# A fused attention and MoE kernel: maxima as bias in the head, another load order, and every third weight pair converted twice

## The chip, the cores and the metric

The kernel runs on one core of a Trainium2 chip. The metric is device time in microseconds. Before the change it is 929.2 us, the median of three runs (927.67 to 930.06).

## The reference, cut to what matters

```python
def _attn_ref(q_l, k_l, v_l, q_g, k_g, v_g):      # B 4, H 8, Sl 512, Sg 32, D 64
    s_g = scale * q_g @ k_all.T                   # 32 global queries see all 544 keys
    out_g = sm(s_g) @ v_all
    s_ll = where(|i - j| <= 32, scale * q_l @ k_l.T, -1e9)
    s_l = concat([scale * q_l @ k_g.T, s_ll])     # local queries: 32 global keys and a band
    out_l = sm(s_l) @ v_all                       # sm subtracts the row's maximum
    return concat([out_g, out_l])

def reference(...):
    x = attention, reshaped to (2176, 512)
    xn = x / sqrt(mean(x * x) + 1e-6) * rms_g
    y = (silu(xn @ w_gate) * (xn @ w_val)) @ w_out       # d_ff 1536
    h = relu(y @ w_in)
    return (s * h * h + b) @ moe2_w_out                  # d_ff 2048
```

## The kernel before, in words

The 2176 tokens are cut into five groups (GROUPS: three of 512 tokens, two of 320). A group goes through two phases. Phase 1 has 12 blocks f, each with a gate block `g`, a value block `v` and an output block `o`; phase 2 has 16 blocks, each with an input block `i` and an output block `p`. A block of weights is 128x512 and costs 12 matmuls of 512 columns (`mm3`, L705 to L708: a product is formed of three, high times high, high times low, low times high part). The blocks lie in 34 pairs (PAIRS) in the order of BLOCKS: pair 0 holds g0 and v0, pair 1 g1 and v1, pair 2 o0 and g2, pair 3 v2 and o1, and so on.

Weights come as raw 8-byte numbers, 1 MB a pair (`load_raw`, L166). In the first group each pair is converted: `conv_begin` (L184) makes the scaled high word on ScalarE (L192) and, on ScalarE and VectorE (L202, L203) or on VectorE alone (`halves`, L197 and L199), the low bits, clamps (L205) and merges them (L206); `conv_end` (L210) makes the high part on ScalarE (L213) and the low part on VectorE (L214), starts the next raw load and stores the finished pair of 1 MB to memory (L217). The later groups load the finished pairs (L242). `used` (L232) is called when a block has been used up; at the end of a pair it converts the pair four further on (C_LEAD) or loads the one five further on (W_LEAD). There are seven buffers for finished pairs and four for raw ones.

The attention of the first batch, four units (a unit is two heads), is done in the head by `start` (L572), the others between the weight matmuls in steps that a planner emits (`sched`, `tick`, `emit_step`; a step has a due time in TensorE's time). In `start`, `S_(u)` computes scores, masks the band's ends (L313), takes the maximum (L314), subtracts it (L315) and takes the exponential (L320); `T_(u)` transposes and copies; `V_(u)` multiplies with the values, forms the shares (`shares`, L333: L336 to L338), squares and sums them (L649, L652, L653). `fill` (L614) issues matmuls of ones whose result nobody reads. `first_norm` (L540) computes the norm, scales (L553, L555), transposes (L562) and writes x in two parts (L567, L568). Then the main stream of weight matmuls starts (L706).

The order on an engine in the head is set by hand with `in_line` (L173), which makes each instruction of a list follow the one before it on its engine; elsewhere in the first group a scheduler sets it from priorities (`hp`) and dependences. From the second group on, TensorE, ScalarE and VectorE keep the program's order (L766). SP issues all transfers, in the order of its queue:

```python
        ld_qk(0)
        nc.sync.dma_start(out=ct, in_=cst)
        ld_qk(1)
        ld_qk(2)
        ld_v(0)
```

Unit steps behind the head are in `pair_steps` (L345): `st_s` scores, `st_e` exponentials, `st_t` transposes, `st_v` values and shares. In phase 2 a block's result goes through relu (L812), `t` (L813), the high part of h (L815) and its remainder (L816), into one of two buffers; two PSUM banks ("m") take turns for the blocks `g`, `v` and `i`.

Of the kernel before, what the change touches and what calls it, by code (L numbers as in the profile page):

```python
# [70 lines left out]
C_LEAD = 4  # L71


@with_exitstack
def attn_moe_kernel(ctx: ExitStack, tc: tile.TileContext, q, k, v, w, cst, out):
# [39 lines left out]

    behind = mybir.DependencyInfo(mybir.DependencyClass.NoSync, mybir.DependencyReason.DATA)
# [25 lines left out]
    raws = {}  # L142
# [41 lines left out]
    def conv_begin(n, halves=False):  # L184
# [6 lines left out]
        with hp(20):  # L191
# [9 lines left out]
            else:  # L201
# [4 lines left out]
            d.append(V.scalar_tensor_tensor(out=t, in0=t, scalar=3, in1=e, op0=ALU.logical_shift_left,  # L206
                                            op1=ALU.bitwise_or))
        return g, a, d

    def conv_end(n, g):  # L210
        wn = w_tile(n)
        with hp(40):
            a = A.copy(out=wn[:, :, 0], in_=g)  # L213
            d = V.tensor_tensor(out=wn[:, :, 1], in0=g, in1=wn[:, :, 0].bitcast(F32), op=ALU.subtract)  # L214
        load_raw()
        wsc[n] = dr_p.tile([128, 2, 2, 512], F32, name=f"wsc{n}")
        nc.sync.dma_start(out=wsc[n], in_=wn.bitcast(F32))  # L217
        return a, d

    def conv(n):  # L220
# [5 lines left out]
        conv_end(n, g)  # L226

# [4 lines left out]
    def used(n):  # L232
        left[n] -= 1
        if left[n]:
            return
        del wt[n], left[n]
        if n + C_LEAD < PAIRS:
            conv(n + C_LEAD)
        while PAIRS <= nload[0] <= n + W_LEAD and nload[0] < PAIRS * len(GROUPS):
            m = nload[0]  # L240
            nload[0] += 1
            nc.sync.dma_start(out=w_tile(m).bitcast(F32), in_=wsc[m % PAIRS])  # L242
# [13 lines left out]
    def load_qk(i):  # L256
# [51 lines left out]

    def less_max(bk, pp):
        sv = bk.rearrange("p h (c n) -> p (h c) n", n=128)  # L310
        ends = sv.rearrange("p a (b n) -> p a b n", n=64)[:, :, :, 0:32]
        mx = sm_p.tile([128, 8], F32, tag="mx", name="mx")
        r = [V.tensor_tensor(out=ends, in0=ends, in1=mask, op=ALU.add)]  # L313
# [31 lines left out]
    def pair_steps(i, now):  # L345
# [78 lines left out]
        def st_v(e):  # L424
# [5 lines left out]
            if loc:  # L430
                shares(bk, u_tile(b)[:, :, 128 * (p + e):128 * (p + e) + 128])
# [108 lines left out]
    def first_norm(ss, fill):  # L540
# [9 lines left out]
        for c in range(4):  # L550
            o = ut[0][:, c]
            if c == 3:
                scaled.append(A.mul(out=o, in_=o, mul=r[:, c:c + 1]))  # L553
            else:
                scaled.append(V.tensor_scalar(out=o, in0=o, scalar1=r[:, c:c + 1], scalar2=None, op0=ALU.mult))  # L555
# [16 lines left out]
    def start():  # L572
# [50 lines left out]
        cp, ex, sq, ev, rd, am = {}, {}, {}, {}, {}, {}  # L623

        def S_(u, n=0):
# [16 lines left out]
        def V_(u):  # L642
            bk = banks(("at", "acc1", "acc0", "at")[u])
            in_turn(values(bk, window(u), lambda a, g: pts[u][:, a, 32 * g:32 * g + 32]), True)
            ev[u] = shares(bk, u0[:, :, 128 * u:128 * u + 128])
            j = tmp_p.tile([128, 4, 128], F32, tag="ta", name="s_j")
            uu = u0[:, :, 128 * u:128 * u + 128]
            if u < 2:
                sq[u] = [A.activation(out=j[:, c], in_=uu[:, c], func=AF.Square, accum_out=ss[:, c, u:u + 1])  # L649
                         for c in range(4)]  # L650
            else:
                sq[u] = A.activation(out=j, in_=uu, func=AF.Square)  # L652
                rd[u] = V.tensor_reduce(out=ss[:, :, u], in_=j, axis=mybir.AxisListType.X, op=ALU.add)  # L653
# [22 lines left out]
        g1, a1, d1 = conv_begin(1, True)  # L676
        a1e, d1e = conv_end(1, g1)
        g2, a2, d2 = conv_begin(2)
# [225 lines left out]
```

## Time and profile before

| | |
|---|---|
| median of three runs | 929.2 us |
| the profiled execution | 930.39 us |
| its span, first to last instruction | 928.6 us |
| mean granted TensorE clock | 0.989 |
| matmuls, weight loads | 6946, 6946 |
| VectorE, ScalarE busy | 434.8 us, 387.2 us |
| read from memory, written | 214.60 MB, 40.11 MB |

The profile is of one execution; 1.8 us of its time lie outside the span. Times in the views are microseconds from the span's start. A busy matmul in the rows overlaps the next, so the distance of starts, not the duration, gives the pace. "idle before" names what ended the idle time ahead of an instruction, as the trace's semaphores tell it; "issue" is a wait for nothing that the profile shows.

### The profile page before, as it was taken

How to read it: one execution, taken by the hardware profiler on the slowest of the kernel's cores; microseconds unless marked ns; L12 is line 12 of the kernel's file. 1: busy time of each engine (PE TensorE's matmuls, PEld its weight loads, DVE VectorE, ACT ScalarE, POOL GpSimd, SP SyncE). 2: the span in 40 equal slices, each digit the busy share in tenths (PEclk: the TensorE clock that was granted, in tenths of full speed). 3: DMA queues.
4: the chain of work that ended last, by engine and by line, in shares of the span. 5: the costliest groups of instructions: out<-in, count | busy, mean ns of one | idle time of the engine just before them, and what ended most of it. 6: DMA issues, size and time to landing. Idle time of an engine off the chain costs nothing.

```text
span 928.6 us, 16334 instructions
## 1 busy us (share of the span) xinstructions
PE 910.9 (98%) x6946; PEld 777.3 (84%) x6946; DVE 434.8 (47%) x754; ACT 387.2 (42%) x558; POOL 0.6 (0%) x7
## 2 busy tenths in 40 slices
PE   9799999999999999999999999999999999999998
PEld 6577887878878878888878878887899999999998
DVE  5898889979642242334251332344222235311333
ACT  2797997979424115233214115231232233211322
POOL 0000000000000000000000000000000000000000
PEclk7999999999999999999999999999999999999999
DMA  9999999986976675564585655554588787798880
GB/s 359 404 404 424 365 426 422 395 341 277 393 266 220 257 252 181 211 238 179 181 297 205 235 209 182 179 193 151 194 323 305 277 291 272 248 338 303 289 300 29
DMA packets 43960, 255.77 MB, mean 275 GB/s; under 512 B 5104, under 2 KB 9456, under 8 KB 15984
## 3 DMA queue, kind: packets, MB, share of 16 engines
q1 hardware_dynamic: 43888, 254.73, 73.5%
q8 instruction: 55, 0.90, 0.4%
q14 instruction: 17, 0.14, 0.0%
HBM read 214.60 MB, written 40.11 MB: 274 GB/s over the span
## 4 chain that ended last, share of the span: by engine, by line
PE 92%; ACT 3%; DVE 3%; DMA 1%; issue 1%; SPq 0%; ACTq 0%; DVEq 0%
PE m L706 16%; PE m L707 16%; PE m L708 16%; PE acc L706 12%; PE acc L707 12%; PE acc L708 12%; PE at L289 1%; PE at L329 1%; PE at L324 1%; PE at L374 1%; PE at L408 1%; ACT cv L192 1%; PE at L494 1%; DMA wr<-in_w_dram 1%; DMA s_k<-in_k_dram 1%
## 5 line engine op out<-in xcount | busy, mean ns | idle before, releaser
L707 PE MATMUL acc<-h,wt 128*128 128x512 f32 (+1 forms) x536 | 193.6, 361 | 0.8 <-DVE h L816 0.8
L708 PE MATMUL acc<-h,wt 128*128 128x512 f32 (+1 forms) x536 | 192.4, 359 | 0.0
L706 PE MATMUL acc<-h,wt 128*128 128x512 f32 (+1 forms) x536 | 187.0, 364 | 3.2 <-ACT h L815 2.8
L706 PE MATMUL m<-x,wt 128*128 128x512 f32 (+1 forms) x480 | 174.1, 363 | 0.2 <-ACT sg L783 0.2
L708 PE MATMUL m<-x,wt 128*128 128x512 f32 (+1 forms) x480 | 171.6, 358 | 0.0
L707 PE MATMUL m<-x,wt 128*128 128x512 f32 (+1 forms) x480 | 171.6, 357 | 0.0
L706 PE MATMUL m<-y,wt 128*128 128x512 f32 (+1 forms) x320 | 115.7, 362 | 2.7 <-DVE t L813 2.7
L706 PEld LDWEIGHTS acc<-h,wt 128*128 128x128 f32 x536 | 100.9, 189 | 17.8 <-ACT h L815 4.1
L707 PE MATMUL m<-y,wt 128*128 128x512 f32 (+1 forms) x320 | 115.3, 360 | 0.3 <-DVE y L743 0.3
L708 PE MATMUL m<-y,wt 128*128 128x512 f32 (+1 forms) x320 | 114.9, 359 | 0.0
L707 PEld LDWEIGHTS acc<-h,wt 128*128 128x128 f32 x536 | 101.0, 189 | 14.4 <-DVE h L816 2.1
L708 PEld LDWEIGHTS acc<-h,wt 128*128 128x128 f32 x536 | 101.1, 189 | 12.8
L795 DVE TENSOR_TENSOR a<-sg,m 128x512 f32<-128x512 f32 (+1 forms) x60 | 36.4, 606 | 158.8 <-PE m L708 147.3
L813 DVE SCALAR_TENSOR_TENSOR t<-m,ct,r 128x512 f32<-128x512 f32 (+1 forms) x80 | 53.6, 670 | 119.3 <-ACT r L812 118.9
L706 PEld LDWEIGHTS m<-x,wt 128*128 128x128 f32 x480 | 90.0, 188 | 13.5 <-issue 1.6
L812 ACT ACTIVATE r<-m 128x512 f32<-128x512 f32 (+1 forms) x80 | 42.4, 533 | 140.1 <-PE m L708 139.7
L708 PEld LDWEIGHTS m<-x,wt 128*128 128x128 f32 x480 | 90.1, 188 | 11.6
L707 PEld LDWEIGHTS m<-x,wt 128*128 128x128 f32 x480 | 90.2, 188 | 11.0 <-DVE x L568 0.2
L783 ACT ACTIVATE sg<-m 128x512 f32<-128x512 f32 (+1 forms) x60 | 32.0, 534 | 138.5 <-PE m L708 138.4
L815 ACT ACTIVATE h<-t,ct 128x512 fp32r<-128x512 f32 (+1 forms) x79 | 52.3, 662 | 54.6 <-DVE t L813 49.8
L816 DVE SCALAR_TENSOR_TENSOR h<-t,ct,h 128x512 fp32r<-128x512 f32 (+1 forms) x79 | 53.1, 673 | 46.2 <-ACT h L815 46.2
L153 ACT CAST h<-a 128x512 fp32r<-128x512 f32 (+1 forms) x55 | 30.6, 556 | 94.6 <-DVE a L795 94.6
(159 smaller groups left out, 980.2 us busy)
## 6 DMA issues: line engine op xcount, KB each, us to landing
wt<-wsc SPq DMA_DIRECT2D x136, 1024.0 KB, 4.9
wr<-in_w_dram SPq DMA_DIRECT2D x34, 1024.0 KB, 9.2
wsc<-wt SPq DMA_DIRECT2D x34, 1024.0 KB, 8.8
vr<-in_v_dram SPq DMA_DIRECT2D x12, 1105.0 KB, 8.0
fk<-in_k_dram SPq DMA_DIRECT2D x12, 784.0 KB, 6.3
fq<-in_q_dram SPq DMA_DIRECT2D x12, 272.0 KB, 6.8
out_dram<-z SPq DMA_DIRECT2D x12, 256.0 KB, 5.8
s_v<-in_v_dram SPq DMA_DIRECT2D x2, 1040.0 KB, 8.9
```

The source lines that it names most:

```text
L153: A.copy(out=out_, in_=in_)
L192: mul = lambda: A.mul(out=g, in_=hi.bitcast(F32), mul=W_SC)
L289: mms.append(PE.matmul(bk[32 * g:32 * g + 32, h, 128 * c:128 * c + 128].rearrange("p (a n) -> p a n", a=2), lhsT=qr[x, SG + 32 * i:SG + 32 ...
L706: mms = [PE.matmul(out_, lhsT=wh, rhs=xh, start=first, stop=False), PE.matmul(out_, lhsT=wh, rhs=xl, start=False, stop=False), PE.matmul(o ...
L707: PE.matmul(out_, lhsT=wh, rhs=xl, start=False, stop=False),
L708: PE.matmul(out_, lhsT=wl, rhs=xh, start=False, stop=last)]
L783: recent["A"] = A.activation(out=sg[:, :N], in_=gb[:, :N], func=AF.Silu)
L795: V.tensor_tensor(out=a[:, :N], in0=sg[:, :N], in1=vb[:, :N], op=ALU.mult)
L812: A.activation(out=r[:, :N], in_=hb[:, :N], func=AF.Relu)
L813: V.scalar_tensor_tensor(out=t[:, :N], in0=hb[:, :N], scalar=ct[:, C_S:C_S + 1], in1=r[:, :N], op0=ALU.mult, op1=ALU.mult)
L815: recent["A"] = A.activation(out=h[:, 0, :N], in_=t[:, :N], func=AF.Identity, bias=ct[:, C_B:C_B + 1])
L816: recent["V"] = V.scalar_tensor_tensor(out=h[:, 1, :N], in0=t[:, :N], scalar=ct[:, C_B:C_B + 1], in1=h[:, 0, :N].bitcast(F32), op0=ALU.add ...
```

## The change

- `S_` for units 0, 1 and 2: the subtraction goes; the maximum times -0.125 is the bias of eight exponentials of 128 columns each, which read the scores' bank. No filling stands ahead of unit 2's scores.
- Loads: raw pair 0 is issued behind q and k of unit 1, v of all four units behind q and k of unit 3. Raw pair 2 waits for the 21st value matmul of unit 3 (`vm[3][20]`); raw pair 3 and pair 0's store follow it on SP's queue, and q and k of the next batch follow raw pair 4.
- `V_`: units 0 to 2 are squared whole on ScalarE and summed on VectorE, unit 3 half on each. All four scalings are VectorE's, and the filling ahead of the first transposes is four instead of six.
- The third pair is converted as a whole behind the first silu. The orders of ScalarE and VectorE in the head are written anew.
- Pairs 4, 7, ..., 31 (AGAIN) are not stored in the first group. In the second they are loaded raw again, converted in seven steps that `tick` emits between the others (`conv_steps`), and stored then for the last three groups.
- `st_v`: the shares follow the latest remainder (`recent["V"]`). The planner's first unit step in the first group comes 12 us after the start instead of 10.

```diff
+AGAIN = range(4, PAIRS - 2, 3)
+RAW = list(range(PAIRS)) + [PAIRS + n for n in AGAIN]
...
     def load_raw():
-        n = nraw[0]
-        if n < PAIRS:
+        if nraw[0] < len(RAW):
+            n = RAW[nraw[0]]
             nraw[0] += 1
             wraw[n] = wr_p.tile([128, 2, 512], I64, tag="wr", name="wr")
-            raws[n] = nc.sync.dma_start(out=wraw[n], in_=w[n])
+            raws[n] = nc.sync.dma_start(out=wraw[n], in_=w[n % PAIRS])
...
+    def keep(n, wn):
+        m = n % PAIRS
+        if n == m and m in AGAIN:
+            return
+        wsc[m] = dr_p.tile([128, 2, 2, 512], F32, name=f"wsc{m}")
+        stores[n] = nc.sync.dma_start(out=wsc[m], in_=wn.bitcast(F32))
...
+    def conv_steps(n):
...
+        def end():
+            V.tensor_tensor(out=wn[:, :, 1], in0=g, in1=wn[:, :, 0].bitcast(F32), op=ALU.subtract)
+            load_raw()
+            keep(n, wn)
+
+        return [(lambda: A.mul(out=g, in_=hi.bitcast(F32), mul=W_SC), 0.0),
+                (lambda: A.copy(out=e.bitcast(I16), in_=odd), 1.3),
+                (lambda: V.tensor_scalar(out=g, in0=g, scalar1=-W_HI * W_SC, scalar2=W_HI * W_SC, op0=ALU.max,
+                                         op1=ALU.min), 0.6),
+                (lambda: V.tensor_scalar(out=e, in0=e, scalar1=13, scalar2=-0x7FFFFFF9, op0=ALU.arith_shift_right,
+                                         op1=ALU.bitwise_and), 1.3),
+                (lambda: V.scalar_tensor_tensor(out=t, in0=t, scalar=3, in1=e, op0=ALU.logical_shift_left,
+                                                op1=ALU.bitwise_or), 0.6),
+                (lambda: A.copy(out=wn[:, :, 0], in_=g), 1.3), (end, 1.3)]
...
         if n + C_LEAD < PAIRS:
             conv(n + C_LEAD)
+        elif n + W_LEAD in RAW[PAIRS:]:
+            sched["c"] += conv_steps(n + W_LEAD)
...
             if i < 2:
-                in_line([raws[3], d])
+                in_line([raws[4], d])
...
             if loc:
-                shares(bk, u_tile(b)[:, :, 128 * (p + e):128 * (p + e) + 128])
+                r = shares(bk, u_tile(b)[:, :, 128 * (p + e):128 * (p + e) + 128])
+                if "V" in recent:
+                    in_line([recent["V"], r])
...
         ld_qk(1)
+        load_raw()
         ld_qk(2)
-        ld_v(0)
         ld_qk(3)
-        ld_v(1)
-        ld_v(2)
-        load_raw()
-        ld_v(3)
+        for u in range(4):
+            ld_v(u)
...
+        def S_(u):
             bk = banks(("acc0", "at", "acc1", "acc0")[u])
-            if n:
-                fill(bk[:, 0], n)
             in_turn(first_scores(bk, raw[u][0], raw[u][1]), True)
-            am[u] = less_max(bk, P[u % 3])
-            ex[u] = expo(P[u % 3])
+            if u == 3:
+                am[u] = less_max(bk, P[u % 3])
+                ex[u] = [expo(P[u % 3])]
+                return
+            sv = bk.rearrange("p h (c n) -> p (h c) n", n=128)
+            mx = sm_p.tile([128, 8], F32, tag="mx", name="mx")
+            am[u] = [mask_ends(sv), V.tensor_reduce(out=mx, in_=sv, axis=mybir.AxisListType.X, op=ALU.max),
+                     V.tensor_scalar(out=mx, in0=mx, scalar1=-0.125, scalar2=None, op0=ALU.mult)]
+            ex[u] = [A.activation(out=P[u % 3][:, a], in_=sv[:, a], func=AF.Exp, scale=0.125, bias=mx[:, a:a + 1])
+                     for a in range(8)]
...
-            S_(2, 1)
+            S_(2)
...
-            roots, r, scaled, xa, xd = first_norm(sm, lambda b: fill(b, 6))
+            roots, r, scaled, xa, xd = first_norm(sm, lambda b: fill(b, 4))
...
-        g2, a2, d2 = conv_begin(2)
-        in_line([ex[0], ex[1]] + cp[0] + [ex[2]] + cp[1] + [ex[3]] + cp[2] + sq[0] + [a0[0]] + cp[3] + sq[1]
-                + [a1[0], a0e, sq[2], a2[0], sq[3], a1e] + roots + [scaled[3]] + xa + [a2[1]])
-        in_line([am[0], am[1], am[2], am[3], ev[0], d0[0], d0[1], d0[2], d0[3], ev[1], d1[0], d1[1], ev[2], d1[2], d1[3], ev[3],
-                 rd[2], rd[3], sums, r[0], r[1]] + scaled[:3] + [d0e] + xd + [d1e, d2[0], d2[1], d2[2]])
-        begun.append(d2[2])
-        ending.append(lambda: conv_end(2, g2))
+        tc.add_manual_dep(raws[2].ins, vm[3][20].ins.name, landed, reason="after")
+        in_line([raws[2], raws[3], stores[0]])
+        in_line(ex[0] + a0 + ex[1] + cp[0] + ex[2] + cp[1] + [a0e] + ex[3] + cp[2] + cp[3] + sq[0] + sq[1] + sq[2] + a1
+                + sq[3] + roots + xa + a1e)
+        in_line(am[0] + d0[:2] + am[1] + [d0[2]] + am[2] + [d0[3]] + am[3] + [d0e, ev[0], ev[1], ev[2]] + rd[0]
+                + [d1[0], ev[3]] + rd[3] + rd[1] + rd[2] + [sums, d1[1], r[0], r[1]] + scaled + [d1[2]] + xd
+                + [d1[3], d1e[0], d1[4], d1e[1]])
+        begun.append(d1e[1])
+
+        def third_pair(sg):
+            g2, a2, d2 = conv_begin(2)
+            in_line([a1e[1], sg] + a2)
+            in_line([d1e[1]] + d2)
+            conv_end(2, g2)
+
+        ending.append(third_pair)
...
         if s["q"] and s["t"] >= s["ok"] and not s["hold"] and (gap or len(s["q"][0]) < 3):
             emit_step()
+            s["cok"] = max(s["cok"], s["t"] + (3.0 if gap else 0.7))
+        elif s["c"] and s["t"] >= s["cok"]:
+            s["c"].pop(0)[0]()
+            s["cok"] = s["t"] + (s["c"][0][1] if s["c"] else 0.0)
...
-            sched["ok"] = sched["t"] + (0.0 if gi else 10.0)
+            sched["ok"] = sched["t"] + (0.0 if gi else 12.0)
...
             if ending:
-                in_line([recent["A"], ending.pop(0)()[0]])
+                ending.pop(0)(recent["A"])
                 conv(C_LEAD - 1)
```

## Rows read from the trace of the kernel before

**Rows 1.** The page, part 1: engine, busy us, share of the span, instructions.

```profile
PE 910.9 (98%) x6946; PEld 777.3 (84%) x6946; DVE 434.8 (47%) x754; ACT 387.2 (42%) x558; POOL 0.6 (0%) x7
```

**Rows 2.** Stages: busy us of PE, PEld, DVE, ACT, POOL; clock, DMA share, GB/s.

```profile
18.20:28.30 10.10, 6.98 (x230) 6.11 (x231) 7.36 (x11) 6.92 (x16) 0.00 (x0) 1.00 1.02 417
...
31.90:42.00 10.10, 8.32 (x53) 4.38 (x45) 8.86 (x21) 9.54 (x15) 0.00 (x0) 1.00 1.02 416
...
42.00:100.00 58.00, 57.42 (x375) 45.56 (x374) 51.74 (x71) 48.97 (x49) 0.00 (x0) 1.00 1.01 409
...
250.00:440.00 190.00, 190.00 (x1430) 154.73 (x1429) 67.81 (x119) 57.70 (x89) 0.00 (x0) 1.00 0.64 231
```

**Rows 3.** TensorE's waits, 42 to 245 us: total us, times, longest us.

```profile
PE m L706 <- DVE t L813: 2.7, 2, 2.1
```

**Rows 4.** Timelines of ScalarE, VectorE and TensorE around 206 us: start, duration.

```profile
198.87 0.60 ACT L812 ACTIVATE r<-m 128x512 f32<-128x512 f32 x1 [0.95 <-PE m L708]
...
205.50 0.17 DVE L336 TENSOR_SCALAR rs<-at 128x8 f32<-128x8 f32 x1 [1.52 <-PE at L408]
...
207.62 0.74 DVE L813 SCALAR_TENSOR_TENSOR t<-m,ct,r 128x512 f32<-128x512 f32 x1
...
208.41 0.50 PE L706 MATMUL m<-y,wt 128*128 128x512 f32 x1 [2.11 <-DVE t L813]
```

**Rows 5.** Chain that ended last, 196 to 214 us: start, duration, what.

```profile
209.75 0.43 PE m L707
...
213.02 0.92 PE acc L706 x4
```

**Rows 6.** Timeline of TensorE in the head and at the main stream's start.

```profile
27.40 0.30 PE L329 MATMUL acc<-s_v,ptf 128*32 128x65 f32 x3 [3.12 <-issue]
...
33.68 0.22 PE L329 MATMUL at<-s_w,ptf 128*32 128x65 f32 x1 [1.54 <-issue]
...
34.03 5.42 PE L615 MATMUL acc<-ones 128*128 128x512 f32 x12
...
41.96 0.71 PE L706 MATMUL m<-x,wt 128*128 128x512 f32 x2
```

**Rows 7.** DMA queues, 27.4 to 33.68 us: packets, MB, share of 16 engines.

```profile
q8 instruction: 1, 0.02, 1.1%
```

**Rows 8.** Timeline of VectorE and ScalarE in the head.

```profile
8.67 1.22 DVE L315 TENSOR_TENSOR pm<-acc,mx 128x1024 f32<-128x1024 f32 x1
...
9.93 1.06 ACT L320 ACTIVATE pm<-pm 128x1024 f32<-128x1024 f32 x1 [7.91 <-DVE pm L315]
...
26.00 0.30 ACT L649 ACTIVATE s_j<-u 128x128 f32<-128x128 f32 x1
...
34.95 0.16 DVE L336 TENSOR_SCALAR rs<-at 128x8 f32<-128x8 f32 x1
...
37.85 0.30 ACT L542 ACTIVATE r<-ss,epsc 128x4 f32<-128x4 f32 x1
```

**Rows 9.** Timeline behind the main stream's start: first silu, third pair's first matmuls.

```profile
47.31 0.60 ACT L783 ACTIVATE sg<-m 128x512 f32<-128x512 f32 x1 [2.93 <-PE m L708]
...
54.06 1.21 PE L706 MATMUL acc<-h,wt 128*128 128x512 f32 x4 [0.34 <-ACT h L153]
```

**Rows 10.** Groups by line, 40 to 260 us: count, busy us, mean ns, idle before.

```profile
L202 ACT COPY ce<-wr 128x2048 int16<-128x2048 int16 x31 | 58.8, 1896 | 0.0
...
L206 DVE SCALAR_TENSOR_TENSOR cv<-cv,ce 128x1024 int32<-128x1024 int32 x32 | 39.1, 1223 | 0.5
L192 ACT ACTIVATE cv<-wr 128x1024 f32<-128x1024 f32 x32 | 36.9, 1154 | 0.0
L213 ACT CAST wt<-cv 128x1024 fp32r<-128x1024 f32 x32 | 33.6, 1050 | 6.5 <-DVE cv L206 6.5
...
L205 DVE TENSOR_SCALAR cv<-cv 128x1024 f32<-128x1024 f32 x32 | 22.1, 690 | 5.7 <-ACT cv L192 5.6
```

**Rows 11.** Groups by line on ScalarE, 250 to 440 us, columns as above.

```profile
L815 ACT ACTIVATE h<-t,ct 128x512 fp32r<-128x512 f32 x13 | 9.4, 724 | 11.4 <-DVE t L813 11.4
```

More of the change, by code (lines that the diff above doesn't have):

```diff
@@ L141, in attn_moe_kernel @@
     wt, wraw, wsc, left = {}, {}, {}, {}
-    raws = {}
+    raws, stores = {}, {}
     nraw = [0]
@@ L205, in conv_begin, with conv_end @@
             d.append(V.tensor_scalar(out=g, in0=g, scalar1=-W_HI * W_SC, scalar2=W_HI * W_SC, op0=ALU.max, op1=ALU.min))
-            d.append(V.scalar_tensor_tensor(out=t, in0=t, scalar=3, in1=e, op0=ALU.logical_shift_left,
-                                            op1=ALU.bitwise_or))
+            for x in parts(split):
+                d.append(V.scalar_tensor_tensor(out=t[:, x], in0=t[:, x], scalar=3, in1=e[:, x],
+                                                op0=ALU.logical_shift_left, op1=ALU.bitwise_or))
         return g, a, d
-    def conv_end(n, g):
+    def keep(n, wn):
[4 more added lines that the diff above has]
+        stores[n] = nc.sync.dma_start(out=wsc[m], in_=wn.bitcast(F32))
+    def conv_end(n, g, split=False):
         wn = w_tile(n)
+        a, d = [], []
         with hp(40):
-            a = A.copy(out=wn[:, :, 0], in_=g)
-            d = V.tensor_tensor(out=wn[:, :, 1], in0=g, in1=wn[:, :, 0].bitcast(F32), op=ALU.subtract)
+            for x in parts(split):
+                a.append(A.copy(out=wn[:, x, 0], in_=g[:, x]))
+                d.append(V.tensor_tensor(out=wn[:, x, 1], in0=g[:, x], in1=wn[:, x, 0].bitcast(F32), op=ALU.subtract))
         load_raw()
-        wsc[n] = dr_p.tile([128, 2, 2, 512], F32, name=f"wsc{n}")
-        nc.sync.dma_start(out=wsc[n], in_=wn.bitcast(F32))
-        return a, d
+        keep(n, wn)
+        return (a, d) if split else (a[0], d[0])
     def conv(n):
@@ L241, in used @@
             nload[0] += 1
+            if m in RAW:
+                continue
             nc.sync.dma_start(out=w_tile(m).bitcast(F32), in_=wsc[m % PAIRS])
@@ L307, in first_scores, with mask_ends @@
         return mms
+    def mask_ends(sv):
+        ends = sv.rearrange("p a (b n) -> p a b n", n=64)[:, :, :, 0:32]
+        return V.tensor_tensor(out=ends, in0=ends, in1=mask, op=ALU.add)
     def less_max(bk, pp):
         sv = bk.rearrange("p h (c n) -> p (h c) n", n=128)
-        ends = sv.rearrange("p a (b n) -> p a b n", n=64)[:, :, :, 0:32]
         mx = sm_p.tile([128, 8], F32, tag="mx", name="mx")
-        r = [V.tensor_tensor(out=ends, in0=ends, in1=mask, op=ALU.add)]
+        r = [mask_ends(sv)]
         V.tensor_reduce(out=mx, in_=sv, axis=mybir.AxisListType.X, op=ALU.max)
@@ L551, in first_norm @@
             o = ut[0][:, c]
[L552 to L555, printed above, removed]
+            scaled.append(V.tensor_scalar(out=o, in0=o, scalar1=r[:, c:c + 1], scalar2=None, op0=ALU.mult))
         X[0] = xy_p.tile([128, 2, HP, NMAX], F32R, tag="x", name="x")
@@ L643, in V_ @@
             bk = banks(("at", "acc1", "acc0", "at")[u])
-            in_turn(values(bk, window(u), lambda a, g: pts[u][:, a, 32 * g:32 * g + 32]), True)
+            vm[u] = values(bk, window(u), lambda a, g: pts[u][:, a, 32 * g:32 * g + 32])
+            in_turn(vm[u], True)
             ev[u] = shares(bk, u0[:, :, 128 * u:128 * u + 128])
-            j = tmp_p.tile([128, 4, 128], F32, tag="ta", name="s_j")
+            j = pg[:, 0:512] if u == 3 else pms[1].rearrange("p a n -> p (a n)")[:, 512 * (u % 2):512 * (u % 2) + 512]
+            j = j.rearrange("p (c n) -> p c n", c=4)
             uu = u0[:, :, 128 * u:128 * u + 128]
-            if u < 2:
+            if u == 3:
                 sq[u] = [A.activation(out=j[:, c], in_=uu[:, c], func=AF.Square, accum_out=ss[:, c, u:u + 1])
[L650 to L653, printed above, removed]
+                         for c in range(2)]
+                rd[u] = [V.scalar_tensor_tensor(out=j[:, c], in0=uu[:, c], scalar=1.0, in1=uu[:, c], op0=ALU.mult,
+                                                op1=ALU.mult, accum_out=ss[:, c, u:u + 1]) for c in range(2, 4)]
+                return
+            sq[u] = [A.activation(out=j, in_=uu, func=AF.Square)]
+            rd[u] = [V.tensor_reduce(out=ss[:, :, u], in_=j, axis=mybir.AxisListType.X, op=ALU.add)]
         acc_p.append(ctx2.enter_context(tc.tile_pool(name="ph", bufs=1, space=PSUM)))
```

22 lines of the change are left out of this document (16 added, 6 removed).

## The prediction

> **What bounds the kernel now.** I read the page first: TensorE is busy for 98% of the span [rows 1]. The table by stage shows that behind the head nothing but TensorE's own work is left over: between 250 and 440 us it is busy for all 190.00 us, ScalarE and VectorE for only 57.70 and 67.81 us [rows 2]. In the first group, up to about 245 us, these two convert the weights and are nearly as full as TensorE (48.97 and 51.74 of 58 us between 42 and 100 us). So time can be won in two places alone: before the main stream of weight matmuls starts (41.96 us [rows 6]), and where TensorE stands still behind that.
>
> For the second place I read TensorE's waits from 42 to 245 us. The longest kind is 2.7 us, for VectorE's `t` on L813 [rows 3]. The timeline around the longest one shows how it comes about [rows 4]. ScalarE has finished a relu at 199.47, so its `t` could run then; but VectorE's next instructions in order are conversion steps and L336, the first step of an attention unit's shares, which waits until 205.50 for TensorE's value matmuls. `t` runs at 207.62, and TensorE, whose two banks are full, stands for 2.11 us until 208.41. Behind that, seven matmuls go at 0.43 us each, against 0.92 us for four, 0.23 each, at the usual pace [rows 5]: the half level of the clock, 1.2 GHz. That is 7 x 0.20 = 1.4 us more, so the whole event costs 3.5 us.
>
> For the first place the timeline of TensorE in the head shows two waits put down to "issue" [rows 6]: 3.12 us until 27.40 in the second unit's value matmuls, and 1.54 us until 33.68. Between the two resumptions lie 6.28 us and 3 + 8 + 64 + 53 = 128 matmuls (three of unit two, the transposes, unit three, unit four so far), and just one instruction transfer of the profile's queue 8 [rows 7]. I read this as instructions that arrive 128 matmuls at a time, no faster than once in 6.3 us while the transfer engines are full (DMA share 1.02 [rows 2]). The fourth unit's last value matmul ends at 33.95; VectorE's shares, sums and norm follow.
>
> **The change, part by part.** *Maxima as bias.* For three units VectorE loses the subtraction of 1.22 us and gains a scaling of eight numbers, 0.16 us as L336: 1.06 us less each [rows 8]. ScalarE's exponential of 1.06 us becomes eight of 128 columns. Their price lies between 1.06 us (same elements, no cost of their own) and 8 x 0.43 = 3.4 us (0.30 us for L542 with a bias from memory on 4 columns, and 0.13 us for 128 columns, an eighth of L320). I take the nearest row, a square of 128 columns, 0.30 us: 2.4 us. So a unit's chain does not get shorter (1.22 + 1.06 = 2.3 us now, 0.16 + 2.4 = 2.6 us then); 3.2 us leave VectorE and 4.0 us come to ScalarE. Both have room before 27 us, since TensorE is the one held there: 0.
>
> *Raw pair third, no filling.* A pair of 1.05 MB takes 2.5 us at 417 GB/s [rows 2], so the third unit's q and k land 2.5 us later, and a filling of about 2 us ahead of its scores goes. The two nearly cancel, and the instruction supply sets the later end, not the scores: 0.
>
> *Raw pairs 2 and 3 held until the last unit's 21st value matmul.* What is loaded ahead of them, 9 MB, takes at least 21.5 us at that rate, so the transfer engines run empty near 25 us. The first issue wait should stay, because its block is asked for while loads still run (two fill matmuls fewer move the boundary by two). The second should go, because its block comes over an empty queue. From 27.4 us on, three units' work is left: 1.3 us of transposes, 1.6 and 1.6 us of values at the half clock that follows such a wait, 0.1 us of handover. That ends near 32.0 instead of 33.95: **-2.0 us** (bounds 0, if the second wait stays, and -3.2, at the full clock). On SP's queue raw pairs 2 to 4, the first store and the next batch's q and k stand behind this hold. Pair 2 lands some 5 us after its issue near 31, and ScalarE wants it at 46; q and k are wanted only after the 12 us that the planner now keeps free.
>
> *Tail to the first matmul.* Today the shares start at 34.95 [rows 8], 1.0 us after the last value matmul, behind a conversion step; from there to the first main matmul it is 7.0 us. New: 0.2 us of handover (-0.8), two products with sums of 0.3 us more, a conversion step that sticks out by 0.2 us beside ScalarE's two small steps, and the fourth scaling on VectorE, 0.2 us: **+0.2 us**. First main matmul: 41.96 - 2.0 + 0.2 = 40.2. Filling: six of them take 5.42 us [rows 6], four 3.6 us; the transposes start some 5.6 us after the last value matmul, so TensorE idles for 2.0 us ahead of the main stream. After the wait of 1.54 us the clock stayed full (1.00 from 31.9 to 42 us [rows 2]), after that of 2.11 us it fell; between 0 and 1.4 us I take the middle: **+0.7 us**.
>
> *Third pair converted wholly behind the first silu.* Today its preparation lies in the head, and TensorE waits 0.34 us for its first use, 12.1 us after the main stream's start [rows 9]. New, from the silu's start 5.35 us after that point: 0.60 + 1.90 + 1.15 us on ScalarE, 0.69 + 1.22 us on VectorE, 1.05 us on ScalarE [rows 9, 10] make 12.0, with handovers 12.3 us. TensorE's 48 matmuls of the first two pairs are through after 48 x 0.227 = 10.9, with a bank wait of 0.4 us 11.3. It waits 1.0 us instead of 0.3: **+0.6 us** (bounds 0, if the first silu comes earlier, and +3.9, if the next pair's copy of 1.90 us goes first and the clock falls for 1.4 us).
>
> *Shares forced behind the latest remainder.* The new line in the value step puts `t` and L816 ahead of L336 on VectorE, which is the event of 3.5 us: **-3.5 us** (bounds -3.5 and 0, if the new order builds another one).
>
> *Every third pair kept raw.* Ten stores of 1 MB leave the first group, ten loads of equal size change their source. No wait of TensorE there is for a transfer: 0. The second group gets ten conversions, 10 x 4.1 us on ScalarE and 10 x 3.8 us on VectorE (two steps of 0.69 as L205, two of 1.22 as L206 [rows 10]), in a stage where both are idle for over 120 us of 190. The relu's chain (0.60, 0.74, 0.72, 0.74 us [rows 4, 11]) takes 2.8 us, and 24 matmuls, 5.4 us, pass before TensorE needs its end; one copy of 1.90 us in the way fits into the 2.6 us left: 0. Without that cover see the third rival.
>
> Sum: -2.0 + 0.2 + 0.7 + 0.6 - 3.5 = **-4.0 us**. The profiled execution lasted 930.39 us, 1.2 us over the median of 929.2; the sum on it gives 926.4, on the median **925.2 us**. Differences under 0.3%, 2.8 us, can't be told from none: faster means under 926.4, slower over 932.0.
>
> **The rivals.** (1) *The event comes back in another place.* The first group is ordered by a scheduler, and every moved instruction moves its list; with one event of 3.5 us the time is 928.7. For it: 2.7 us of waits are of this one kind, on a VectorE nearly full. Against: the forced order covers shares now as it did scores. Chance 0.24. (2) *Both issue waits go.* The fourth unit then ends near 28, 4 us sooner than in my sum: 921.2. For it: two fill matmuls fewer, and a queue that empties early. Against: the loads before 25 us are as dense as now. Chance 0.10. The Trainium skill ("Runtime: NRT & Kernel Launch", Instruction fetch mechanics) says that an engine fetches its next block while it executes the current one, and that this is mostly hidden; by it this rival would be the rule, at 921.2, and the trace's waits of 3.12 and 1.54 us speak against it. (3) *Slower: the second group's conversions get into the relu chain.* Four of the ten fall into its second half. If a copy of 1.90 us holds up the relu and a step of 1.22 us each holds up `t` and the remainder, the delay is 4.3 us against a cover of 2.6: 1.7 us, four times 6.8 us, and if the clock falls behind two of them 2.8 us more: 925.2 + 9.6 = 934.8. It decides once both engines are hit for the same block. Against it: both reach these steps early, with half their time idle. Chance 0.16.
>
> **Numbers.** Forecast 0.50, rivals 0.24, 0.10 and 0.16. The range of 920.5 to 931.5 holds the forecast with its bounds and rivals 1 and 2, and leaves out rival 3. Most of the forecast (0.45) and rival 2 are faster, the rest of it (0.05) and rival 1, less a hundredth, are the same; rival 3 and that hundredth are slower: 0.55, 0.28, 0.17. The forecast's own range is 922 to 928.
>
> **What would show it.** First main matmul near 40 us; one issue wait left in the head, ending near 27; the third pair's cast done 12 us after the start; no matmuls at 0.43 us between 200 and 245 us; still no waits of TensorE between 250 and 440 us. The prediction is wrong if the main stream starts after 42 us, if such waits appear in the second group, or if a wait for `t` of over a microsecond is still there.

## The result and the profile after

The changed kernel takes 936.08 us, the median of six runs (933.87 to 936.92), against 929.63 us for six runs of the kernel before (927.67 to 930.75). The ratio is 1.0065, with a 95% interval of 1.0052 to 1.0078: slower by 0.65%, where 925.2 us was forecast. The profiled execution took 935.92 us, 5.5 us more than that of before, and its span is 934.1 us.

Part 1 of the page after the change, to be held against [rows 1]:

```profile
PE 912.3 (98%) x6940; PEld 778.6 (83%) x6940; DVE 468.9 (50%) x802; ACT 426.3 (46%) x598; POOL 0.6 (0%) x7
```

The page hardly shows it. But for six fill matmuls TensorE has as many instructions; ScalarE and VectorE have 39 and 34 us more, about what ten second conversions take. What the page hides, the count of main matmuls shows. Both kernels run the same 4080 of them (816 in the first group, of which 432 in its first phase), so the start of the k-th can be compared. The table is worked out from the starts in the two traces; the last column says what lies in the stretch. The "turn of the phases" is where the first group goes from phase 1 to phase 2.

| main matmuls | before, us | after, us | difference | what is in it |
|---|---|---|---|---|
| start of the 0th | 41.96 | 38.61 | -3.35 | the head |
| 0 to 60 | 14.99 | 18.53 | +3.54 | q and k late, third pair late |
| 60 to 432 | 96.81 | 96.85 | +0.04 | |
| 432 to 480 | 13.88 | 17.10 | +3.22 | turn of the phases, at 161 us |
| 480 to 600 | 30.97 | 30.97 | 0.00 | |
| 600 to 640 | 15.17 | 14.83 | -0.34 | the event of [rows 4], still there |
| 640 to 1000 | 90.28 | 90.31 | +0.03 | |
| 1000 to 1632 | 157.88 | 160.22 | +2.34 | second group |
| 1632 to 4079 | 463.02 | 463.07 | +0.05 | last three groups |
| sum | | | +5.53 | |

**The head is better than forecast.** Of the 3.12 and 1.54 us put down to "issue" in [rows 6], 0.31 us is left, and TensorE then idles for 2.11 us ahead of the transposes. Its timeline there (start, duration):

```profile
29.87 0.24 PE L375 MATMUL at<-s_r,ptf 128*32 128x65 f32 x1 [0.31 <-issue]
...
36.03 2.83 PE L607 MATMUL acc<-ct,u 128*128 128x128 f32 x16 [2.11 <-DVE u L600]
38.61 0.71 PE L772 MATMUL m<-x,wt 128*128 128x512 f32 x2
```

In this execution TensorE's clock was at its half level until 24.9 us, in the kernel before only until 18.2 us. One stage of the changed kernel (busy us of PE, PEld, DVE, ACT, POOL; clock, DMA share, GB/s):

```profile
7.80:24.90 17.10, 16.37 (x324) 14.50 (x325) 12.21 (x16) 11.66 (x31) 0.00 (x0) 0.50 1.00 406
```

**Behind it, TensorE waits again.** Its waits from 42 to 245 us (total us, times, longest); [rows 3] has the one kind of before that was over 2 us in total:

```profile
PE m L772 <- DVE t L879: 3.9, 2, 2.0
PE m L772 <- DVE a L861: 1.6, 1, 1.6
PE m L773 <- DVE y L809: 0.8, 1, 0.8
PE acc L774 <- DVE wt L230: 0.5, 1, 0.5
PE acc L772 <- ACT wt L229: 0.5, 1, 0.5
```

The second row is the first place. The timeline of SP's queue shows when the next batch's q and k are issued, that of VectorE what stands behind their landing, that of ScalarE the silu that L861 needs:

```profile
29.47 1.28 SPq L174 DMA_DIRECT2D wr<-in_w_dram  x3
30.84 0.52 SPq L222 DMA_DIRECT2D wsc<-wt  x1
31.41 0.43 SPq L308 DMA_DIRECT2D fq<-in_q_dram  x1
...
45.72 0.17 DVE L403 COPY qf<-fq 64x32 f32<-64x32 f32 x1 [0.73 <-DMA fq<-in_q_dram]
...
48.29 0.37 DVE L403 COPY qf<-fq 64x32 f32<-64x32 f32 x2 [1.95 <-DMA fq<-in_q_dram]
48.69 0.69 DVE L861 TENSOR_TENSOR a<-sg,m 128x512 f32<-128x512 f32 x1
...
44.17 0.59 ACT L849 ACTIVATE sg<-m 128x512 f32<-128x512 f32 x1
...
51.88 1.05 ACT L229 CAST wt<-cv 128x1024 fp32r<-128x1024 f32 x1 [0.45 <-DVE cv L213]
```

Three raw pairs and a store, 4 MB, go ahead of q and k, which land at 45 to 48 us. VectorE runs its list in order and stands for 0.73 and 1.95 us at two copies of 64x32; the silu has been done since 44.76, but `a` of L861 starts at 48.69. So TensorE waits 1.60 us, every conversion step behind moves, and the third pair's cast ends at 52.93, for which TensorE waits again (the last two rows of the waits).

The two waits for `t` (L879) are the turn of the phases and the event that was to go. Of the first, VectorE's timeline; copies of the next q, an attention unit's maximum (L424) and a conversion step (L230) stand ahead of the `t`:

```profile
160.89 0.17 DVE L403 COPY qf<-fq 64x32 f32<-64x32 f32 x1 [0.17 <-PE at L421]
160.98 0.71 DVE L424 TENSOR_REDUCE gm<-at 128x1 f32<-128x544 f32 x1
...
162.00 1.22 DVE L230 TENSOR_TENSOR wt<-cv,wt 128x1024 fp32r<-128x1024 f32 x1
163.13 0.75 DVE L879 SCALAR_TENSOR_TENSOR t<-m,ct,r 128x512 f32<-128x512 f32 x1
```

And of the second, ScalarE's and VectorE's (compare [rows 4]):

```profile
198.71 0.60 ACT L878 ACTIVATE r<-m 128x512 f32<-128x512 f32 x1 [1.73 <-PE m L774]
...
199.95 0.75 DVE L882 SCALAR_TENSOR_TENSOR h<-t,ct,h 128x512 fp32r<-128x512 f32 x1 [0.94 <-ACT h L881]
...
209.62 0.17 DVE L382 TENSOR_SCALAR rs<-at 128x8 f32<-128x8 f32 x1 [2.54 <-PE at L454]
...
210.74 0.74 DVE L879 SCALAR_TENSOR_TENSOR t<-m,ct,r 128x512 f32<-128x512 f32 x1
```

The relu ends at 199.31 and its `t` could follow, but the shares' first step L382, waiting for TensorE until 209.62, is ahead of it, as before. The new line does order L382 behind "the latest remainder", and that is the L882 at 199.95, which belongs to the block before. The `t` that is wanted is one block younger. TensorE behind the two waits, and in the second group:

```profile
163.93 0.50 PE L772 MATMUL m<-y,wt 128*128 128x512 f32 x1 [1.95 <-DVE t L879]
...
211.53 0.50 PE L772 MATMUL m<-y,wt 128*128 128x512 f32 x1 [2.00 <-DVE t L879]
...
444.96 0.50 PE L772 MATMUL acc<-h,wt 128*128 128x512 f32 x1 [0.76 <-ACT h L881]
445.75 0.50 PE L773 MATMUL acc<-h,wt 128*128 128x512 f32 x1 [0.28 <-DVE h L882]
```

Half clock follows both 2 us waits (columns as above):

```profile
164.80:168.20 3.40, 3.40 (x10) 2.62 (x9) 2.16 (x4) 3.40 (x3) 0.00 (x0) 0.50 0.98 307
212.60:216.00 3.40, 3.40 (x10) 2.64 (x9) 2.04 (x4) 3.40 (x4) 0.00 (x0) 0.50 0.99 406
```

In the second group a wait of 0.76 and 0.28 us stands at 444 us, where steps of a second conversion and of an attention unit stand ahead of the relu chain on both engines. On ScalarE the conversion's cast (L265) and L548 are ahead of the relu, whose block ends near 438.8; on VectorE L550 and the conversion's last step (L253) are ahead of `t`, whose relu is done at 441.41:

```profile
438.70 1.05 ACT L265 CAST wt<-cv 128x1024 fp32r<-128x1024 f32 x1 [1.95 <-DVE cv L263]
439.66 1.26 ACT L548 ACTIVATE x<-at,ct 128x512 fp32r<-128x512 f32 x2
440.81 0.60 ACT L878 ACTIVATE r<-m 128x512 f32<-128x512 f32 x1
...
440.95 1.41 DVE L550 SCALAR_TENSOR_TENSOR x<-at,ct,x 128x512 fp32r<-128x512 f32 x2 [2.28 <-ACT x L548]
442.28 1.21 DVE L253 TENSOR_TENSOR wt<-cv,wt 128x1024 fp32r<-128x1024 f32 x1
443.41 0.74 DVE L879 SCALAR_TENSOR_TENSOR t<-m,ct,r 128x512 f32<-128x512 f32 x1
```

The relu is 2.0 us late and `t` another 2.0 us.

### The profile page after: what moved, and what is told of

Its sections match the earlier page's. It is cut to its first block, busy times and chain, and to the rows that moved or that the text cites. A ratio compares the mean times of both kernels' runs of the same rounds, so it can differ in the third digit from the quotient of the medians.

```text
span 934.1 us, 16390 instructions
## 1 busy us (share of the span) xinstructions
PE 912.3 (98%) x6940; PEld 778.6 (83%) x6940; DVE 468.9 (50%) x802; ACT 426.3 (46%) x598; POOL 0.6 (0%) x7
## 4 chain that ended last, share of the span: by engine, by line
PE 86%; DVE 7%; ACT 3%; DMA 3%; issue 1%; SPq 0%; ACTq 0%; DVEq 0%
PE m L772 15%; PE m L773 15%; PE m L774 15%; PE acc L773 11%; PE acc L772 11%; PE acc L774 11%; DMA fq<-in_q_dram 2%; PE at L375 2%; PE at L332 1%; PE at L370 1%; DVE t L879 1%; PE at L420 1%; DMA s_r<-in_k_dram 1%; ACT h L881 1%; PE at L454 1%
## 5 line engine op out<-in xcount | busy, mean ns | idle before, releaser
L773 PEld LDWEIGHTS acc<-h,wt 128*128 128x128 f32 x536 | 101.0, 188 | 15.5 <-DVE h L882 3.0
L861 DVE TENSOR_TENSOR a<-sg,m 128x512 f32<-128x512 f32 (+1 forms) x60 | 36.3, 605 | 143.6 <-PE m L774 132.1
L879 DVE SCALAR_TENSOR_TENSOR t<-m,ct,r 128x512 f32<-128x512 f32 (+1 forms) x80 | 53.5, 668 | 101.3 <-ACT r L878 100.7
L772 PEld LDWEIGHTS m<-x,wt 128*128 128x128 f32 x480 | 90.0, 188 | 15.6 <-DVE a L861 2.0
L882 DVE SCALAR_TENSOR_TENSOR h<-t,ct,h 128x512 fp32r<-128x512 f32 (+1 forms) x79 | 53.0, 671 | 47.5 <-ACT h L881 47.5
L772 PEld LDWEIGHTS m<-y,wt 128*128 128x128 f32 x320 | 60.8, 190 | 12.3 <-DVE t L879 4.5
```

Of the source, the lines that this page charges most:

```text
L772: mms = [PE.matmul(out_, lhsT=wh, rhs=xh, start=first, stop=False), PE.matmul(out_, lhsT=wh, rhs=xl, start=False, stop=False), PE.matmul(o ...
L773: PE.matmul(out_, lhsT=wh, rhs=xl, start=False, stop=False),
L861: V.tensor_tensor(out=a[:, :N], in0=sg[:, :N], in1=vb[:, :N], op=ALU.mult)
L879: V.scalar_tensor_tensor(out=t[:, :N], in0=hb[:, :N], scalar=ct[:, C_S:C_S + 1], in1=r[:, :N], op0=ALU.mult, op1=ALU.mult)
L882: recent["V"] = V.scalar_tensor_tensor(out=h[:, 1, :N], in0=t[:, :N], scalar=ct[:, C_B:C_B + 1], in1=h[:, 0, :N].bitcast(F32), op0=ALU.add ...
```

## The experiments

The theory, A in the expectations: each place has a cause of its own that can be taken away alone. The rival, B, puts the same time on something else (the scheduler's lists, that is the order it gives to each engine's instructions, the clock, the transfers); what it gives stands in each expectation. All kernels compute the whole result. Edits are against the changed kernel. Their line numbers differ by up to two from those of the changed kernel. A run without an interval is one execution, and the clock in the head alone moves that by over 2 us, so those are read by the stretches of the table above, not by their totals. Where no edit reaches, the stretches agree well: from the 816th to the 1000th matmul all 14 traces take 48.55 to 48.58 us.

**Place 1 (x1): q and k ahead of raw pairs 3 and 4.**

```diff
             if i < 2:
-                in_line([raws[4], d])
+                in_line([raws[2], d])
+                if t is kr and i == 1:
+                    in_line([d, raws[3]])
```

> Alone changed against the changed kernel: q and k of the next batch's first two units are loaded ahead of raw pair 3 instead of behind raw pair 4. Theory A (VectorE stands in front of the copies of q until their load lands, and so delays the gate times value product and the third pair): the q copies run right behind the second pair's conversion (near 45 us), the wait of TensorE for the product of L861 (1.6 us) goes, and the main stream is 1.5 to 3 us further ahead at its 60th matmul than the changed kernel (54.1 to 55.6 us instead of 57.1). Rival B (the third pair's chain is too long in itself): the 60th matmul stays within 0.7 us of 57.1.

Measured 933.26 us. From 0 to 60 it takes 16.69 us: 1.84 us of the 3.54 are back, and the wait for L861 is gone. The 60th matmul starts at 55.98, just outside what A expected. One wait of TensorE has replaced the others (waits, 42 to 260 us):

```profile
PE acc L774 <- ACT wt L229: 1.9, 1, 1.9
```

It is the third pair's cast, now the last to come. VectorE's and ScalarE's timelines show it held up behind its input, by ScalarE's other work, the next silu the last of it:

```profile
49.06 1.23 DVE L213 SCALAR_TENSOR_TENSOR cv<-cv,ce 128x1024 int32<-128x1024 int32 x1
...
51.51 0.62 ACT L851 ACTIVATE sg<-m 128x512 f32<-128x512 f32 x1
52.00 1.06 ACT L229 CAST wt<-cv 128x1024 fp32r<-128x1024 f32 x1
```

So q and k are half of this place, the third pair the other half.

**Place 2 (x2): the planner's start, 12 back to 10.**

```diff
-            sched["ok"] = sched["t"] + (0.0 if gi else 12.0)
+            sched["ok"] = sched["t"] + (0.0 if gi else 10.0)
```

> Alone changed: the planner's first unit step is free 10 us after the start again, not 12. Theory A (the later unit steps put the scores' maximum and the q copies ahead of t at the turn of the phases): the stand of 1.95 us at 162 us shrinks to about the 0.6 us of the kernel before and no half clock follows, 2.5 to 3.3 us less between the 432nd and the 480th matmul. Rival B (the order at the turn comes from the conversions, not from the planner): that stretch costs the same 3.2 us as in the changed kernel.

Measured 933.79 us. From 432 to 480 it takes 13.83 us, as before (13.88): A. But the new lists have a wait of 1.1 us for a silu at 94 us, so 60 to 432 takes 1.35 us more. And of the 3.22 us at the turn 1.6 are the half clock, which does not come each time: x1, y2 and y3, whose planner still starts at 12, take 15.5 to 15.6 us there. In x1 TensorE has the same wait of 1.95 us and the clock stays full behind it:

```profile
162.00:166.00 4.00, 3.21 (x14) 2.68 (x15) 3.09 (x7) 3.52 (x4) 0.00 (x0) 1.00 0.98 306
```

**Second conversions off (x3).**

```diff
-AGAIN = range(4, PAIRS - 2, 3)
+AGAIN = range(0)
```

> Alone changed: no pair is converted a second time; all 34 are stored in the first group and loaded finished afterwards, as before. Theory A (the second conversions cost TensorE only the waits at 373 and 444 us): the second group takes 2.0 to 2.4 us less (no waits between 250 and 640 us but those of the kernel before), and the first 60 main matmuls are as late as in the changed kernel, within 0.7 us. Rival B (the ten stores fewer are what the first group lives on): the first group is slower by over 2 us, with waits of TensorE for converted weights.

Measured 935.96 us. From 1000 to 1632 it takes 157.88 us, exactly as before: the 2.34 us belong to the second conversions. From 0 to 60 it takes 17.80 us, 0.73 less than the changed kernel. The total does not follow, because the first group's lists are others: the event at 206 us is gone and a larger wait stands at the turn of the phases, with another ahead of it (waits, 42 us on):

```profile
PE m L772 <- DVE t L879: 4.6, 1, 4.6
PE acc L772 <- ACT x L156: 1.8, 1, 1.8
```

The first group ends 2.5 us later than in the changed kernel, as B has it, but 2.4 of that are the head's, at another clock, and its waits for converted weights are the same two of 0.5 us: B is not borne out.

**The shares' order off (x4).**

```diff
-                r = shares(bk, u_tile(b)[:, :, 128 * (p + e):128 * (p + e) + 128])
-                if "V" in recent:
-                    in_line([recent["V"], r])
+                shares(bk, u_tile(b)[:, :, 128 * (p + e):128 * (p + e) + 128])
```

> Alone changed: the shares no longer follow the latest remainder. Theory A (the forced order names the remainder of the block before the one whose t is late, so it does nothing for the stand at 209 us): the stand of 2.0 us and the half clock behind it are there as in the changed kernel, and the total is within 1.5 us of it. Rival B (the forced order moves the event and has made it as large as it is): the stand is under 1 us and the total is 2 to 4 us less.

Measured 936.3 us; 600 to 640 takes 14.83 us, the same as with the line, with the same wait of 2.0 us for `t`. The line does nothing: it names a remainder that has long run.

**Place 1 whole (y1): the third pair prepared in the gaps of the second.** With the first edit, and its cast alone left behind the silu:

```diff
+        g2, a2, d2 = conv_begin(2)
...
-                + sq[3] + roots + xa + a1e)
+                + sq[3] + roots + xa + [a2[0], a1e[0], a2[1], a1e[1]])
...
-                + [d1[3], d1e[0], d1[4], d1e[1]])
-        begun.append(d1e[1])
+                + [d1[3], d1e[0], d1[4], d1e[1]] + d2)
+        begun.append(d2[-1])
...
-            in_line([a1e[1], sg] + a2)
-            in_line([d1e[1]] + d2)
-            conv_end(2, g2)
+            in_line([sg, conv_end(2, g2)[0]])
```

> Against the run with q and k first (x1): the third pair's two preparing steps on ScalarE go into the gaps around the second pair's casts, VectorE's three behind them, and only the cast stands behind the first silu. Theory A (what x1 still loses between the 12th and the 60th matmul, 1.7 us, is the third pair's chain behind the silu): TensorE's wait of 1.9 us for that cast goes, and from the first to the 60th main matmul it takes 14.9 to 15.4 us, as in the kernel before (15.0), where x1 takes 16.7. Rival B (ScalarE as a whole is late there, by the third and fourth pair together): the wait moves to the fourth pair and the stretch takes over 16.2 us.

Measured 930.1 us. From 0 to 60 it takes 14.83 us, less than before (14.99). So place 1 is 1.84 us for q and k and 1.86 us for the third pair's order, 0.16 more in all than the change had lost there. Not all of it lasts: from 60 to 432 this order takes 97.48 us, 0.63 more than the changed kernel. At the turn it takes 15.41 us.

**Six second conversions, all in the group's first part (y2).**

```diff
-AGAIN = range(4, PAIRS - 2, 3)
+AGAIN = range(4, 20, 3)
```

> Alone changed against the changed kernel: six pairs instead of ten are converted again, those whose steps fall into the first phase of the second group. Theory A (the second conversions cost where they meet a relu's chain, in the second phase): the waits near 373 and 444 us go and the stretch from the 1000th to the 1632nd main matmul takes under 158.2 us (before 157.9, changed kernel 160.2). Rival B (each conversion costs something): about 0.24 us for each of the six, over 159.2 us.

Measured 932.78 us; 1000 to 1632 takes 158.40 us instead of 160.22, just above A's 158.2. The wait near 444 us is gone, one of 0.2 us near 373 stays. Whether the number or the place of the conversions counts is not told apart.

**The event at 206 (y3): unit steps behind the block's first matmuls.** In the first group's second phase no step is emitted within them:

```diff
-            tick()
+            if gi or b[0] != "i":
+                tick()
```

> Alone changed against the changed kernel: in the first group's second phase the planner emits its steps only behind a block's own relu, t and h, not between its input matmuls, so that the forced order of the shares names the remainder of the very block whose t was late. Theory A (the forced order took hold one block too early): no stand of 2 us for t near 209 us and no half clock behind it; the stretch from the 600th to the 640th matmul takes about 11.5 us, 3.3 us less than in the changed kernel (14.8). Rival B (VectorE has too much work there in any order): a wait for t of over a microsecond is there at another place between 195 and 245 us.

Measured 933.02 us; 600 to 640 takes 11.17 us, 4.0 less than before: the event with its half clock is gone, and no wait for `t` of over a microsecond has come between 195 and 245 us. New waits of 0.9 us (for L550) and 0.3 us (for L548) stand at 253 us, which with what follows cost 1.7 us between 640 and 1000.

**All five edits together**, in one execution (y4) and timed in eleven (z0).

> The changed kernel with q and k first, the third pair in the gaps, the planner at 10 us, six pairs converted again and the steps behind. If the five causes add up: first main matmul at 38.5 to 41 us as in the runs so far, the 60th 15.0 to 15.5 us later, no more than 0.5 us lost at the turn of the phases, 3.3 us won near 209 us, under 0.4 us lost in the second group: 4 to 7 us less than the kernel before in the same call. Rival: the scheduler makes another stand of 3 us or more in the first group, and it is within 3 us of the kernel before.

> The kernel with all five cures again, timed against the kernel before. By its one look it ended 4.1 us ahead of the profile of before: 2 to 5 us faster in the medians, 0.2 to 0.5%. Rival: the head's start, which lay between 38.5 and 41 us in the looks so far, decides, and it is within 1.5 us of the kernel before.

The single execution took 926.68 us; timed it is 926.95 us, the median of 11 runs (926.19 to 928.5), against 929.22 us of 15 runs (928.19 to 930.39), a ratio of 0.9978 with an interval of 0.9969 to 0.9987. So five edits bring back what the change lost, and it beats the kernel before by 2.3 us, 0.2%, as z0's expectation had it. y4's own expectation missed: the kernel before took 928.9 us beside it, so it is 2.2 us less and not 4 to 7, and both the turn of the phases and the second group (0.51 us lost) are over their bounds. The stretches of y4: 14.83 us from 0 to 60, 15.43 from 432 to 480, 11.26 from 600 to 640, 158.39 from 1000 to 1632. The turn of the phases still costs 1.55 us, with the planner at 10: in these lists TensorE waits there for other instructions (waits, 150 to 172 us):

```profile
PE m L773 <- DVE y L810: 1.6, 1, 1.6
PE m L772 <- DVE t L880: 1.0, 1, 1.0
```

y1, with the planner at 12, takes 15.41 us there, y4 with 10 takes 15.43. So the planner's start is the cause only in the order in which it was tried alone.

**All five, without any second conversions (z1)** (`AGAIN = range(0)`).

> All cures, and no pair converted a second time. Theory A (the stores left out win nothing, since no wait of TensorE is for a transfer): the second group loses nothing and the end of the first group (816th matmul) is within 1.5 us of that with six pairs (250.9), unless the scheduler makes a new stand, which the waits would name. Rival B (the stores stand in SP's queue ahead of raw loads and these come late): waits for converted weights (L229, L230) between 60 and 200 us, over 2 us in all.

Measured 934.53 us. The second group loses nothing (157.88 us), as A has it, but the first ends 9.0 us later than with six pairs (816th matmul at 259.9 instead of 250.9), the new stand that A had set aside. B's place was another: at 228 us TensorE waits 5.1 us for a converted weight, half clock behind it. Waits of TensorE, and ScalarE and VectorE around it:

```profile
PE acc L772 <- ACT wt L229: 5.1, 1, 5.1
```

```profile
229.27 1.89 ACT L208 COPY ce<-wr 128x2048 int16<-128x2048 int16 x1
...
232.72 1.03 ACT L229 CAST wt<-cv 128x1024 fp32r<-128x1024 f32 x1
...
226.40 1.68 DVE L538 TENSOR_SCALAR u<-u,r 128x512 f32<-128x512 f32 x4
...
230.08 1.22 DVE L213 SCALAR_TENSOR_TENSOR cv<-cv,ce 128x1024 int32<-128x1024 int32 x1
```

The pair's chain stands in order behind an attention unit's norm and scaling on VectorE (L538), its cast behind the next pair's copy on ScalarE. That is late work of the two engines, not a transfer that is waited for. Whether the six extra stores bring it about, or only the order of these lists, stays open.

**All five, raw pair 2 not held (z2)** (the line with `vm[3][20]` left out).

> All cures, without the hold of raw pair 2. Theory A (the hold is what lets the last instruction blocks of the head come early): issue waits of 3.5 to 5 us in the head instead of 1.9, and the first main matmul 1.5 to 3 us later than 38.5 to 41. Rival B (the hold does nothing, the half clock until 22 us sets the head): first main matmul within 1 us of 38.5 at the same clock.

Measured 926.86 us. Two issue waits come back (waits, 0 to 42 us), and the main stream starts at 41.51 us, against 38.50 in y4, where the clock rose at the same time (21.8 us):

```profile
PE acc L377 <- issue: 1.9, 1, 1.9
PE at L377 <- issue: 1.7, 1, 1.7
```

At this clock the hold brings 3.0 us in the head, by one execution of each; the half clock behind the first of the two waits (28.6 to 32.0 us) is part of it. At the end 0.45 us of it is left. 1.6 us went at the turn of the phases, which in these lists takes 13.84 us (432 to 480), and 1.6 us in the clock behind the wait of 1.8 us that all these kernels have near 640 us. It stayed full here (1.00 from 632 to 640 us), and fell in y4:

```profile
636.20:639.60 3.40, 3.40 (x10) 2.63 (x9) 0.75 (x1) 0.48 (x1) 0.00 (x0) 0.50 0.18 70
```

**All five, the maximum subtracted in all four units (z3).**

```diff
-            if u == 3:
+            if u >= 0:
                 am[u] = less_max(bk, P[u % 3])
```

> All cures, with the maxima of all four units subtracted on VectorE and one exponential for each unit, as before. Theory A (a unit's chain is as long either way, and TensorE is what the head waits for): first main matmul within 1 us of that with the biases (38.5 to 41, by the clock of the run). Rival B (VectorE, which the biases relieve of 3.2 us, sets the head): 1.5 to 3.2 us later.

Measured 926.7 us. The main stream starts at 40.07 us, 1.6 us behind y4 and 1.5 us behind the changed kernel, whose clock rose at the same time as here (24.9 us), so nearer to B; at the end it is 0.3 us behind y4, again with a full clock behind the wait near 640 us. So the biases bring at most 1.6 us in the head. No difference at the end can be told.

## Why the prediction was wrong

The forecast was -4.0 us, measured is +5.5 us in the profiled executions and +6.4 us in the medians. By its own terms:

- **Holding the raw pairs, -2.0 us, with the tail +0.2 and the restart +0.7.** The direction was right. In the profiled execution the three together brought -3.35 us instead of -1.1: the last value matmul starts near 30.1 us instead of 33.88 (where its row ends at 34.10, not at 33.95), both issue waits are all but gone, which is rival 2's mechanism at a smaller price, and the clock stayed full behind the 2.11 us of idling, against 0.7 us taken as the middle. Part of that is luck of the clock. I had said that the first wait stays, because its block is asked for while loads still run. In the five runs with the clock full from 17 us, the nearest to the kernel before (18.2 us), it does: 2.6 to 3.1 us, ending at 25.6 to 26.7 us, and the second is gone. Their main stream starts at 39.2 to 41.1 us, 0.9 to 2.7 us ahead of the kernel before, around the 40.2 of the forecast. Where the clock rose near 22 us the first wait is 0.9 to 1.5 us, where it rose at 24.9 us 0.5 us or none. As I read it, a TensorE at half clock comes to that block later, over emptier queues: the DMA share from 24 to 28 us is 0.24 in the changed kernel, 1.02 in the kernel before. z2 confirms the hold with 3.0 us at the late clock; at the early one it was not taken out.
- **"q and k are wanted only after the 12 us that the planner now keeps free": this step failed.** The scores want them then, but their first use is a small copy in VectorE's order, 7 us after the main stream starts. I had named the queue behind the hold and not asked who reads what stands in it first. x1: 1.84 us.
- **Third pair, +0.6 us (0 to +3.9).** Mis-sized: 1.86 us (y1 against x1), inside its bounds. The chain was summed as if nothing stood between its parts; with q and k first its cast still waits 1.7 us on ScalarE (from 50.29 to 52.00) behind the next pair's first step (1.17 us), L156 and the second silu. It is the kind of delay that I had priced at the upper bound, but not the copy of 1.90 us named there, which goes behind the cast (52.93).
- **Shares behind the latest remainder, -3.5 us: "the new line puts `t` and L816 ahead of L336" failed.** -0.34 us measured, and x4 shows the line without effect. I read which instruction was in the way, and not which block's remainder is the latest at the time when the line is emitted. y3 shows that the 4 us can be had, 2.3 of them net of the new waits at 253 us.
- **The planner's 12 us** had no term of its own but as a cover. It moved the first group's lists, and the turn of the phases lost 3.22 us, 1.6 of them to a half clock that other runs with the same wait did not get; x2 gave all of it back. This is rival 1 (the event elsewhere), with the old event and a new one beside it, so up to nearly twice its price of 3.5 us.
- **Ten conversions in the second group, 0 us.** 2.34 us, shown by x3. Mechanism and sign were rival 3's, at one block near 444 us (1.6 us with the slow restart) and two small places near 373 and 425, not at four blocks: the chain of that block is 4.0 us late against the cover of 2.6. "One copy of 1.90 us in the way fits into the 2.6 us left" left out that both engines can be hit for the same block, and that an attention unit's steps (1.26 and 1.41 us) then stand in the way beside the conversion's (1.05 and 1.21 us).
- **Maxima as bias, 0 us.** Eight exponentials take 2.17 us, where 2.4 was taken from the nearest row:

```profile
8.88 2.17 ACT L679 ACTIVATE pm<-acc,mx 128x128 f32<-128x128 f32 x8 [6.87 <-DVE mx L678]
```

  z3 puts the gain in the head at no more than 1.6 us, by one execution; at the end 0.3 us is left.
- **"What would show it".** Two of the three signs of being wrong came: a wait for `t` of over a microsecond is still there, and waits appear in the second group.

## What to carry to other kernels

When a load is moved back in a queue, look for the first instruction that reads it in each engine's order, however small: a copy of 0.17 us held up a full VectorE by 1.95 us. An order written against "the latest" of something is only as good as what the latest is when the line is emitted; name the instruction itself. Where one part of a change moves a scheduler's list, compare the kernels by the start of the k-th matmul, and try the parts one by one: here four local losses of 1.8 to 3.2 us and a head 3.4 us shorter lay under a total of 5.5, and an older event worth 4 us had stayed.

## What the runs showed of the hardware

The head's time depends on when the granted clock rises. In the 12 profiles with the raw pair held the main stream started between 38.5 and 41.1 us. With the clock at its half level until 21.8 to 24.9 us, the waits put down to "issue" were 0.3 to 2.1 us; in the five runs where it was full from 16.8 to 17.6 us they were 2.6 to 3.1 us, and half clock followed. z0's profile is one of these:

```profile
PE acc L377 <- issue: 3.1, 1, 3.1
```

```profile
17.60:27.90 10.30, 7.22 (x242) 6.21 (x244) 7.25 (x11) 6.66 (x16) 0.00 (x0) 1.00 0.73 292
27.90:31.30 3.40, 3.40 (x129) 3.23 (x120) 1.63 (x6) 1.65 (x4) 0.00 (x0) 0.50 0.00 0
```

A TensorE that is faster here only waits longer: the main stream starts at 38.5 to 40.1 us in the seven runs with the late clock, at 39.2 to 41.1 us in the five with the early one. And a wait of 2 us does not always cost the clock: behind 1.95 us at the turn of the phases it fell to 0.50 in the changed kernel and stayed at 1.00 with q and k first.

The Trainium skill ("Runtime: NRT & Kernel Launch", Instruction fetch mechanics) calls the refill of instructions mostly hidden. The runs here agree only in part: 0.3 us of the waits is left in the changed kernel's profile, 1.1 to 3.1 us in the other runs with the hold, and 3.6 us in the one without it.
